# Low part of x^T and state update of the attention tiles: from VectorE subtractions and additions to identity products on TensorE and copies on ScalarE

## The chip, the cores and the metric

One core of one Trainium2 chip runs the whole program in one launch. The metric is device time in microseconds, the median of three runs. TensorE (PE) has a queue of its own for products and can load the next stationary operand while a product runs; VectorE (DVE), ScalarE (ACT) and GpSimd (POOL) each work through one queue in order; SyncE (SP) issues the DMAs.

## The reference, cut to what matters

Three layers follow each other over 1536 tokens of width 320: a gated linear attention, a feed-forward layer with a piecewise activation, and eight gated experts.

```python
for t in range(S):                       # S = 768, B = 2, H = 8, D = 40
    m_new = maximum(f[t] + m, i[t])
    f_stab, i_stab = exp(f[t] + m - m_new), exp(i[t] - m_new); m = m_new
    C = f_stab * C + i_stab * outer(v[t], k[t])
    n = f_stab * n + i_stab * k[t]
    y[t] = sigmoid(o[t]) * (C @ q[t]) / maximum(abs(n @ q[t]), 1)
x = y as [1536, 320]
h = x @ w_in;  g = where(h >= 1, h, where(h <= -1, 0, (h + 1)**2 / 4));  x = g @ w_out
P = exp(x @ w_gate - max), then 8 row and column normalisations
out = sum over e of P[:, e] * (maximum(x @ w1[e], 0) @ w2[e])
```

## The kernel before, in words

The attention runs in 12 tiles of 128 tokens (6 chunks of the sequence times 2 batches; tile t is chunk t // 2 of batch t % 2). A tile is a Python generator, `attn` (L357 to L452), that hands control back after each of its steps: the scaled values (POOL, L365), for each half of the heads the score products (L379), the decay scan (DVE, L383) and its product with the scores (DVE, L385), then the products with the old state (L395) and with the values (L400), then the outer products of this chunk for the new state (L407), then the division (L428 to L433), and at the end the transposes (L446) and the split of x^T.

The large products run in float32r, a one-record form of a float32 product in which an operand keeps fewer bits. So each operand is kept as a high part, rounded to that form, and a low part, the rest: `XH` and `XL` hold x^T so. `split_x` (L112 to L116) makes them from a PSUM bank: ACT copies to `XH`, DVE subtracts `XH` from the bank into `XL`. Products of plain float32 operands run as two records each.

The state `Cst` of a batch is scaled by the chunk's decay on POOL (L412); then two DVE additions, each of 40 partitions by 164 elements (L440), add the outer products from PSUM. In the first chunk two ACT copies (L442) set it.

Tiles 0 and 1 run first, side by side (L481 to L491), with four dummy products (`warm`, L296) after each step of each tile. The feed-forward layer runs in four stages (`STAGES`); the first is tokens 0 to 255, then 256 to 511, on the first half of the hidden width in pieces of 256 columns, and tiles 2 to 7 are worked off inside it; tiles 8 to 11 follow inside the next two stages. How many steps of a tile follow each piece of the layer is set by `RATE`; a tile needs 8 such steps. All through the first two stages the layer's weights arrive as 64-bit floats and are decoded with four DVE instructions each (`decode`, L213 to L220) and split like x^T. The experts follow.

`bank` hands out PSUM banks by tag: two for `at` (scores, values, outer products), one for `ax` (the product with the state, then the transposes of the same tile). The order of the instructions in each engine's queue is set at build time by the framework's planner with its own estimate of durations, not by the order of the program alone; in the trace, dummy products of later steps run ahead of products that had to wait. Inside stages 1 to 3 the attention's PE and DVE instructions are held behind named instructions of the layer.

Of the kernel before, what the change touches and what calls it, by code (L numbers as in the profile page):

```python
# [9 lines left out]
F32R = mybir.dt.float32r  # L10
I32 = mybir.dt.int32
U32 = mybir.dt.uint32
ACTF = mybir.ActivationFunctionType
ALU = mybir.AluOpType
# [20 lines left out]
WA, WG = 4, 2  # L35
PUMP = (0, 2, 4, 5, 6, 7, 10, 12, 13)
GP = 8
RATE = ((3.4, 0), (0, 2.25), (0, 2.25), (2, 2))

STAGES = ((0, (0,), 256), (512, (0, 1), 512), (0, (1,), 512), (1024, (0, 1), 512))  # L40
LAG1, LAG2 = 2, 3
# [7 lines left out]
def mlstm_moe_moe_kernel(  # L49
# [14 lines left out]
    mm = nc.tensor.matmul  # L64
    act = nc.scalar.activation
    vec = nc.vector
# [8 lines left out]
    def bank(tag):  # L75
        n = {"g1": 2, "g2": 3, "at": 2, "ax": 1}[tag]
        return ps.tile([128, 512], F32, name="bk_" + tag, tag=tag, bufs=n)
# [3 lines left out]
    XH = perm.tile([128, 3, NTOK], F32R, name="XH")  # L81
    XL = perm.tile([128, 3, NTOK], F32R, name="XL")
    ident = cst[:, C_ID : C_ID + 128]
    neg_dn = cst[:, C_ND : C_ND + 1]

    def f(ap):
        return ap.bitcast(F32)
# [24 lines left out]
    def split_x(planes, cols):  # L112
        for k, x in planes:
            act(out=XH[:, k, cols], in_=x, func=ACTF.Copy)
        for k, x in planes:
            vec.tensor_tensor(out=XL[:, k, cols], in0=x, in1=f(XH[:, k, cols]), op=ALU.subtract)  # L116
# [9 lines left out]
    with ExitStack() as atx:  # L126
        ap = atx.enter_context(tc.tile_pool(name="ap", bufs=1))
# [153 lines left out]

        g_s = ap.tile([32, L], F32R, name="g_s")
        zer = cst[0:32, 32 : 32 + L]
        m16_r = ap.tile([32, 16], F32R, name="m16_r")
        lend = ap.tile([104, NCH * 8], F32, name="lend")
        gt = ap.tile([128, NCH, 32], F32, name="gt")
        Cst = ap.tile([104, B, 4, 82], F32, name="Cst")
# [12 lines left out]
        for kw in kws:  # L300
            gp.memset(kw, 0.0)
        gp.memset(Cst, 0.0)
        act(out=m16_r, in_=cst[0:32, C_M16 : C_M16 + 16], func=ACTF.Copy)

        def gate_exps(a, b):
# [51 lines left out]
        def attn(t, tags):  # L357
            ta, tb = tags
            c, b = divmod(t, 2)
# [4 lines left out]
            vw = ap.tile([128, 8, 41], F32, name="vw", tag="vw", bufs=2)  # L364
# [3 lines left out]
            kw = kws[t == 1]  # L368
            for hf in range(2):
                gh = G[:, hf * 4 : hf * 4 + 4, :].rearrange("p h t -> p (h t)")  # L370
                gin = gh
                if c == 0:
                    gin = bank(ta)
                    for i in range(4):
                        h = b * 8 + 2 * i + hf
# [11 lines left out]
            if not last:  # L387
                gp.tensor_tensor(
                    out=kw.rearrange("p (i r) d -> p r i d", r=2)[:, :, :, 0:40], in0=kk.rearrange("p (i r) d -> p r i d", r=2),
                    in1=G[:, :, 127:128].rearrange("p (r i) d -> p r i d", r=2).to_broadcast([128, 2, 4, 40]), op=ALU.mult,  # L390
# [10 lines left out]
            sg = ap.tile([128, 384], F32, name="sg", tag="sg", bufs=2)  # L401
            act(out=sg[:, 0:320], in_=kvo_t[:, 648:968], func=ACTF.Sigmoid)
            yield
            if not last:
                pu = bank(ta)
                for pr in range(4):
                    mm(  # L407
                        pu[0:104, pr * 82 : (pr + 1) * 82], kw.rearrange("p h d -> p (h d)")[:, pr * 128 : pr * 128 + 104],
                        vw[:, 2 * pr : 2 * pr + 2, :].rearrange("p a d -> p (a d)"), start=True, stop=True,
                    )  # L410
                if c:
                    gp.tensor_tensor(  # L412
                        out=Cst[:, b, :, :], in0=Cst[:, b, :, :],
                        in1=lend[:, c * 8 + b * 4 : c * 8 + b * 4 + 4].unsqueeze(2).to_broadcast([104, 4, 82]), op=ALU.mult,
                    )
            pav = pa[:, 0:328].rearrange("p (h d) -> p h d", h=8)
            if c:
                hv = ap.tile([128, 8, 41], F32, name="hv", tag="hv")
                vec.tensor_tensor(
                    out=hv, in0=pi[:, 0:328].rearrange("p (h d) -> p h d", h=8),  # L420
                    in1=gt[:, c, 16 + b * 8 : 16 + b * 8 + 8].unsqueeze(2).to_broadcast([128, 8, 41]), op=ALU.mult,
# [13 lines left out]
            if not last:  # L435
                puv = pu[0:104, 0:328].rearrange("p (r d) -> p r d", r=4)
                for par in range(2):
                    rs, es = slice(par * 64, par * 64 + 40), slice(par * 41, par * 41 + 41)
                    if c:
                        vec.tensor_tensor(out=Cst[rs, b, :, es], in0=puv[rs, :, es], in1=Cst[rs, b, :, es], op=ALU.add)  # L440
                    else:
                        act(out=Cst[rs, b, :, es], in_=puv[rs, :, es], func=ACTF.Copy)  # L442
            px = bank(tb)
            act(out=sg[:, 320:384], in_=sg[:, 256:320], func=ACTF.Copy)
            for k in range(3):
                nc.tensor.transpose(px[:, k * 128 : (k + 1) * 128], sg[:, k * 128 : (k + 1) * 128], ident)  # L446
            yield
            split_x([(slice(0, 3), px[:, 0:384].rearrange("p (k t) -> p k t", k=3))], slice(t * 128, (t + 1) * 128))
            if t + 2 < NTILE:
                tiles_in[t + 2] = load_tile(t + 2)  # L450
            done.add(t)
# [4 lines left out]
        def attn_rest():  # L456
            g = attn(2, ("at", "ax"))
            next(g)
            for t in range(2, NTILE):
                n = 0  # L460
                nxt = None
                while next(g, g) is not g:
                    n += 1
                    if n == 6 and t + 1 < NTILE:
                        nxt = attn(t + 1, ("at", "ax"))
                        next(nxt)
                    yield
                g = nxt
# [4 lines left out]
        def pump_w():  # L473
            w_state[0] = next(wjobs, 99)
# [4 lines left out]
        gate_by_token(0, 1)  # L479
        gate_exps(L, S)  # L480
        starts = [attn(0, ("at", "ax")), attn(1, ("g2", "g2"))]  # L481
        step = 0
        while len(done) < 2:
# [88 lines left out]
        for si, (t0, hfs, w) in enumerate(STAGES):  # L572
# [7 lines left out]
            for hf in hfs:  # L580
# [10 lines left out]
                for o in range(0, 512, w):  # L591
                    while len(done) * 128 < t0 + o + w:
                        next(rest)
                    for ff in range(hf * 8, hf * 8 + 8, nf):
# [12 lines left out]
                        if w_state[0] < (9, 18, 18, 18)[si]:  # L607
                            pump_w()
                        credit += nf * RATE[si][hf]
                        while credit >= 1:  # L610
# [98 lines left out]
        for e in range(NE):  # L709
# [3 lines left out]
            for j in range(3):  # L713
# [17 lines left out]
                for i in range(4):  # L731
                    t = j * 4 + i
# [6 lines left out]
                    if e == NE - 1:  # L739
                        c, b = divmod(t, 2)  # L740
# [63 lines left out]
```

## Time and profile before

| | |
|---|---|
| median of 3 runs | 995.2 us (994.61 to 996.29) |
| the profiled execution's own time | 994.85 us |
| its span, first to last instruction | 993.1 us |
| PE busy | 979.6 us (99%) |
| PE weight loads busy | 861.8 us (87%) |
| DVE busy | 470.1 us (47%) |
| ACT busy | 344.8 us (35%) |
| POOL busy | 31.2 us (3%) |

The profile is of one execution. Its busy time of PE is modelled: products overlap in the array, so that records of 0.28 us follow each other every 0.12 us. How much of a stretch PE really needs is better seen in the distance from one product's start to the next. Shares over the whole span mix the attention with the experts, which take the last 690 us.

### The profile page before, as it was taken

The numbers are of one execution on the slowest core, as the hardware profiler recorded it, in microseconds if no ns is written. First come the engines' busy times: TensorE is split into PE (matmuls) and PEld (weight loads), VectorE is DVE, ScalarE is ACT, GpSimd is POOL, SyncE is SP. The second block draws the span as 40 slices with busy tenths as digits, with TensorE's granted clock in tenths as the row PEclk, the third lists the DMA queues.
The fourth block names the chain that finished last, engine by engine and source line by source line (L and its number), as shares of the span: only waits on it lengthen the run. The fifth ranks groups of instructions, "written<-read, shape, count | busy, mean of one in ns | idle before, by whom it ended". The sixth has DMA issues, their size and how long they took to land.

```text
span 993.1 us, 13483 instructions
## 1 busy us (share of the span) xinstructions
PE 979.6 (99%) x5520; PEld 861.8 (87%) x5520; DVE 470.1 (47%) x853; ACT 344.8 (35%) x622; POOL 31.2 (3%) x43
## 2 busy tenths in 40 slices
PE   9999899999999999999999999999999999999998
PEld 5789788887878899999999999989999999999997
DVE  9999977655563644322522432242253234222222
ACT  3743684477773224211411321141132123111111
POOL 2212101000000000000000000000000000000000
PEclk9999999999999999999999999999999999999999
DMA  5865413000132002100400210030021002000000
GB/s 171 263 169 172 143 57 99 12 1 0 47 113 75 1 1 64 54 1 1 117 1 1 74 44 1 7 111 1 1 87 31 1 17 72 1 1 1 27 27 27
DMA packets 42190, 51.91 MB, mean 52 GB/s; under 512 B 3360, under 2 KB 35744, under 8 KB 42128
## 3 DMA queue, kind: packets, MB, share of 16 engines
q1 hardware_dynamic: 42128, 51.05, 17.3%
q8 instruction: 43, 0.70, 0.3%
q14 instruction: 19, 0.16, 0.0%
HBM read 49.03 MB, written 2.01 MB: 51 GB/s over the span
## 4 chain that ended last, share of the span: by engine, by line
PE 89%; DVE 5%; ACT 3%; DMA 1%; issue 1%; SPq 0%; DVEq 0%; ACTq 0%
PE bk_g L124 41%; PE bk_g L704 9%; PE bk_g L706 8%; PE bk_g L705 8%; PE bk_ax L705 3%; PE bk_ax L704 3%; PE bk_ax L706 3%; PE bk_at L400 2%; PE bk_g L296 2%; PE bk_g L559 2%; PE bk_g L558 1%; PE bk_g L557 1%; PE bk_at L379 1%; DMA raw<-in_w_dram 1%; PE bk_g L561 1%
## 5 line engine op out<-in xcount | busy, mean ns | idle before, releaser
L124 PE MATMUL bk_g<-XH,wk 128*128 128x512 f32 (+1 forms) x1240 | 399.8, 388 | 1.6 <-DVE gs L545 1.6
L724 DVE SCALAR_TENSOR_TENSOR lo<-bk_g,hi 128x512 fp32r<-128x512 f32 x192 | 132.6, 691 | 372.6 <-ACT hi L723 371.7
L124 PE MATMUL bk_g<-XL,wk 128*128 128x512 f32 (+1 forms) x744 | 285.4, 384 | 0.0
L723 ACT ACTIVATE hi<-bk_g 128x512 fp32r<-128x512 f32 x192 | 114.9, 599 | 453.2 <-PE bk_g L124 453.0
L124 PEld LDWEIGHTS bk_g<-XH,wk 128*128 128x128 f32 x1240 | 230.6, 188 | 45.1 <-DVE gs L545 2.6
L704 PE MATMUL bk_g<-wf,hi 128*128 128x320 f32 x576 | 177.4, 308 | 1.1 <-ACT hi L723 1.1
L705 PE MATMUL bk_g<-wf,hi 128*128 128x320 f32 x576 | 177.0, 307 | 0.0
L706 PE MATMUL bk_g<-wf,lo 128*128 128x320 f32 x576 | 176.9, 308 | 0.0
L124 PEld LDWEIGHTS bk_g<-XL,wk 128*128 128x128 f32 x744 | 140.0, 188 | 21.4
L704 PEld LDWEIGHTS bk_g<-wf,hi 128*128 128x128 f32 x576 | 108.0, 187 | 8.1 <-ACT hi L723 1.6
L705 PEld LDWEIGHTS bk_g<-wf,hi 128*128 128x128 f32 x576 | 108.1, 188 | 6.3
L706 PEld LDWEIGHTS bk_g<-wf,lo 128*128 128x128 f32 x576 | 107.9, 187 | 0.0
L705 PE MATMUL bk_ax<-wf,hi 128*128 128x320 f32 x192 | 59.1, 308 | 0.0
L704 PE MATMUL bk_ax<-wf,hi 128*128 128x320 f32 x192 | 59.0, 307 | 0.0
L706 PE MATMUL bk_ax<-wf,lo 128*128 128x320 f32 x192 | 58.4, 304 | 0.0
L545 DVE TENSOR_TENSOR gs<-bk_g,gs 128x512 f32<-128x512 f32 x40 | 27.5, 688 | 26.8 <-ACT gs L543 26.4
L541 ACT ACTIVATE gs<-bk_g 128x512 f32<-128x512 f32 x48 | 28.5, 594 | 28.7 <-PE bk_g L124 28.1
L738 DVE SCALAR_TENSOR_TENSOR acc<-bk_g,P,acc 128x320 f32<-128x320 f32 x63 | 30.8, 545 | 15.3 <-PE bk_g L706 15.3
L531 DVE TENSOR_TENSOR wf<-raw,wf 128x640 fp32r<-128x640 f32 x32 | 26.3, 826 | 20.7 <-ACT wf L530 20.5
L704 PEld LDWEIGHTS bk_ax<-wf,hi 128*128 128x128 f32 x192 | 36.1, 188 | 0.0
L706 PEld LDWEIGHTS bk_ax<-wf,lo 128*128 128x128 f32 x192 | 36.1, 188 | 0.0
L705 PEld LDWEIGHTS bk_ax<-wf,hi 128*128 128x128 f32 x192 | 35.9, 187 | 0.0
(198 smaller groups left out, 999.6 us busy)
## 6 DMA issues: line engine op xcount, KB each, us to landing
raw<-in_w_dram SPq DMA_DIRECT2D x32, 320.0 KB
raw<-in_w_dram SPq DMA_DIRECT2D x32, 256.0 KB
kvo_t<-in_kvo_dram SPq DMA_DIRECT2D x12, 484.0 KB
raw<-in_w_out_dram SPq DMA_DIRECT2D x8, 640.0 KB
raw<-in_w_in_dram SPq DMA_DIRECT2D x8, 512.0 KB
raw<-in_w_dram SPq DMA_DIRECT2D x64, 64.0 KB
qk<-in_qk_dram SPq DMA_DIRECT2D x24, 160.0 KB
G<-g_d SPq DMA_DIRECT2D x5, 512.0 KB
```

The source lines that it names most:

```text
L124: return [mm(dst, a, b, start=i == 0, stop=i == len(seq) - 1) for i, (a, b) in enumerate(seq)]
L296: mm(to, wz, wz[:, 0:1].to_broadcast([128, 512]), start=True, stop=True)
L400: mm(pa[:, h * 41 : (h + 1) * 41], A[h % 2][:, h // 2, :], vw[:, h, :], start=True, stop=True)
L531: vec.tensor_tensor(out=wf[:, fs, 320:640], in0=rs[n], in1=f(wf[:, fs, 0:320]), op=ALU.subtract)
L541: act(out=t, in_=pg, func=ACTF.Relu, scale=-1.0, bias=1.0)
L545: dve_at.append(vec.tensor_tensor(out=g, in0=pg, in1=t, op=ALU.max))
L704: mm(pp[i], hi[:, ts], wf[:, ff, 0:320], start=st, stop=False)
L705: mm(pp[i], hi[:, ts], wf[:, ff, 320:640], start=False, stop=False)
L706: mm(pp[i], lo[:, ts], wf[:, ff, 0:320], start=False, stop=sp)
L723: act(out=hi, in_=pg, func=ACTF.Relu)
L724: vec.scalar_tensor_tensor(out=lo, in0=pg, scalar=0.0, in1=f(hi), op0=ALU.max, op1=ALU.subtract)
L738: vec.scalar_tensor_tensor(out=acc[:, t, :], in0=pp[i], scalar=P[:, t, e : e + 1], in1=acc[:, t, :], op0=ALU.mult, op1=ALU.add)
```

## The change

Three things are made in another way, for each attention tile:

- The low part of x^T. The transposes and the ACT copy to `XH` stay. After one more hand-over of control, three plain float32 products of `sg` with the identity write x^T into the same bank again, a float32r product of the negated identity (`nid`, new, made once by ACT) with `XH` is added to it, and ACT copies the bank to `XL`.
- The update of the state, from the second chunk on. The decayed state is multiplied by the identity into the bank of the outer products as the first product of the group, the four outer products are added to it, and ACT copies the sum back in two pieces. The scaling on POOL now stands ahead of these products in the program.
- A tile has one step more (9 in place of 8 after the first), and `RATE` is raised to 3.75 and 2.5 steps. In the start each step brings its four dummy products for each tile. The dummies inside the tiles are unchanged.

```diff
-RATE = ((3.4, 0), (0, 2.25), (0, 2.25), (2, 2))
+RATE = ((3.75, 0), (0, 2.5), (0, 2.5), (2, 2))
@@
+        nid = ap.tile([128, 128], F32R, name="nid")
@@
+        act(out=nid, in_=ident, func=ACTF.Copy, scale=-1.0)
@@ attn
                 pu = bank(ta)
-                for pr in range(4):
-                    mm(
-                        pu[0:104, pr * 82 : (pr + 1) * 82], kw...[:, pr * 128 : pr * 128 + 104],
-                        vw[:, 2 * pr : 2 * pr + 2, :]..., start=True, stop=True,
-                    )
                 if c:
                     gp.tensor_tensor(
                         out=Cst[:, b, :, :], in0=Cst[:, b, :, :],
                         in1=lend[...]..., op=ALU.mult,
                     )
+                    mm(pu[0:104, 0:328], ident[0:104, 0:104], Cst[:, b].rearrange("p r d -> p (r d)"), start=True, stop=False)
+                for pr in range(4):
+                    mm(
+                        pu[0:104, pr * 82 : (pr + 1) * 82], kw...[:, pr * 128 : pr * 128 + 104],
+                        vw[:, 2 * pr : 2 * pr + 2, :]..., start=c == 0, stop=c == 0 or pr == 3,
+                    )
@@
                     rs, es = slice(par * 64, par * 64 + 40), slice(par * 41, par * 41 + 41)
-                    if c:
-                        vec.tensor_tensor(out=Cst[rs, b, :, es], in0=puv[rs, :, es], in1=Cst[rs, b, :, es], op=ALU.add)
-                    else:
-                        act(out=Cst[rs, b, :, es], in_=puv[rs, :, es], func=ACTF.Copy)
+                    act(out=Cst[rs, b, :, es], in_=puv[rs, :, es], func=ACTF.Copy)
@@
             yield
-            split_x([(slice(0, 3), px[:, 0:384].rearrange("p (k t) -> p k t", k=3))], slice(t * 128, (t + 1) * 128))
+            ts, p3 = slice(t * 128, (t + 1) * 128), px[:, 0:384].rearrange("p (k t) -> p k t", k=3)
+            act(out=XH[:, :, ts], in_=p3, func=ACTF.Copy)
+            yield
+
+            for k in range(3):
+                mm(px[:, k * 128 : (k + 1) * 128], sg[:, k * 128 : (k + 1) * 128], ident, start=k == 0, stop=False)
+            mm(px[:, 0:384], nid, XH[:, :, ts], start=False, stop=True)
+            act(out=XL[:, :, ts], in_=p3, func=ACTF.Copy)
```

## Rows read from the trace of the kernel before

**Rows 1.** The page's head: span, then busy time, share and instructions of an engine.
```profile
span 993.1 us, 13483 instructions
PE 979.6 (99%) x5520; PEld 861.8 (87%) x5520; DVE 470.1 (47%) x853; ACT 344.8 (35%) x622; POOL 31.2 (3%) x43
```

**Rows 2.** Busy time of each engine by stretch, up to the attention's end.
```profile
core 0: us, PE busy (x) PEld busy (x) DVE busy (x) ACT busy (x) POOL busy (x), PEclk, DMA share, GB/s
0.00:36.30 36.30, 35.10 (x202) 21.45 (x202) 34.19 (x66) 17.36 (x35) 6.99 (x17) 1.00 0.64 183
36.30:118.60 82.30, 77.82 (x604) 70.70 (x603) 77.44 (x150) 39.84 (x80) 19.45 (x20) 0.98 0.64 188
118.60:141.90 23.30, 21.87 (x98) 17.81 (x98) 22.27 (x43) 21.59 (x43) 0.00 (x0) 1.00 0.22 71
141.90:175.00 33.10, 31.64 (x189) 27.14 (x188) 21.69 (x37) 15.91 (x28) 4.76 (x6) 1.00 0.30 90
175.00:230.20 55.20, 55.20 (x286) 46.26 (x285) 31.32 (x56) 32.35 (x57) 0.00 (x0) 1.00 0.01 4
```

**Rows 3.** Groups on PE in 36.3 to 118.6 us: line, form, count, busy, mean.
```profile
L124 PE MATMUL bk_g<-XH,wk 128*128 128x256 f32 x80 | 18.0, 304 | 0.0
L124 PE MATMUL bk_g<-XL,wk 128*128 128x256 f32 x48 | 14.1, 298 | 0.0
L379 PE MATMUL bk_at<-qk 104*128 104x128 f32 x96 | 12.8, 281 | 0.0
L400 PE MATMUL bk_at<-vw,A 128*128 128x41 f32 x96 | 11.9, 277 | 0.1
...
L296 PE MATMUL bk_at<-wz 128*128 128x512 bf16 x24 | 6.4, 380 | 0.2 <-DVE A L385 0.2
...
L296 PE MATMUL bk_g<-wz 128*128 128x512 bf16 x16 | 5.5, 412 | 0.8 <-DVE XL L547 0.8
...
L446 PE MATMUL bk_ax<-cst,sg 128*128 128x128 f32 x18 | 3.6, 285 | 0.9 <-DVE sg L433 0.9
```

**Rows 4.** Chain of work, 0 to 130 us: start, us, engine, tile, line, records.
```profile
81.50 0.89 PE bk_at L379 x8
...
82.63 0.33 PE bk_ax L446 x3
...
84.54 0.85 PE bk_ax L395 x8
85.39 0.99 PE bk_g L124 x8
...
88.23 0.77 PE bk_at L407 x8
...
105.63 0.87 PE bk_at L296 x4
106.50 1.73 PE bk_at L400 x16
...
116.06 0.47 PE bk_g L124 x2
```

**Rows 5.** Waits of PE's products, 36.3 to 118.6 us: total, times, longest.
```profile
PE bk_g L557 <- ACT XH L546: 2.1, 2, 1.9
PE bk_ax L446 <- DVE sg L433: 0.9, 2, 0.5
```

**Rows 6.** Copies and subtractions out of bank `ax`: min/median/max ns.
```profile
L114 ACT ACTIVATE XH<-bk_ax x11: 491/491/493, 34.8 to 211.7; 128x384 fp32r<-128x384 f32 x11
L116 DVE TENSOR_TENSOR XL<-bk_ax,XH x11: 531/549/558, 36.3 to 212.2; 128x384 fp32r<-128x384 f32 x11
```

**Rows 7.** Writers of the state: min/median/max ns, first and last start.
```profile
L440 DVE TENSOR_TENSOR Cst<-bk_at,Cst x16: 307/326/331, 53.5 to 174.4; 40x164 f32<-40x164 f32 x16
L412 POOL TENSOR_TENSOR Cst<-Cst,lend x8: 728/732/1202, 42.4 to 172.7; 104x328 f32<-104x328 f32 x8
L442 ACT ACTIVATE Cst<-bk_at x2: 304/306/307, 27.8 to 28.1; 40x164 f32<-40x164 f32 x2
```

More of the change, by code (lines that the diff above doesn't have):

```diff
@@ L405, in attn @@
                 pu = bank(ta)
-                for pr in range(4):
-                    mm(
-                        pu[0:104, pr * 82 : (pr + 1) * 82], kw.rearrange("p h d -> p (h d)")[:, pr * 128 : pr * 128 + 104],
-                        vw[:, 2 * pr : 2 * pr + 2, :].rearrange("p a d -> p (a d)"), start=True, stop=True,
-                    )
                 if c:
@@ L414, in attn @@
                         in1=lend[:, c * 8 + b * 4 : c * 8 + b * 4 + 4].unsqueeze(2).to_broadcast([104, 4, 82]), op=ALU.mult,
+                    )
+                    mm(pu[0:104, 0:328], ident[0:104, 0:104], Cst[:, b].rearrange("p r d -> p (r d)"), start=True, stop=False)
+                for pr in range(4):
+                    mm(
+                        pu[0:104, pr * 82 : (pr + 1) * 82], kw.rearrange("p h d -> p (h d)")[:, pr * 128 : pr * 128 + 104],
+                        vw[:, 2 * pr : 2 * pr + 2, :].rearrange("p a d -> p (a d)"), start=c == 0, stop=c == 0 or pr == 3,
                     )
```

## The prediction

> **What bounds the kernel now.** I began with the head of the page [rows 1]: PE is busy for 979.6 of 993.1 us. For the experts I take that as it stands, since nothing of the change reaches them. For the attention I asked for the busy time by stretch [rows 2]. The reader is to see two engines that are nearly full at the same time in 36.3 to 118.6 us, the first stage of the layer with tiles 2 to 7 in it: DVE is busy for 77.44 of 82.3 us, PE for a modelled 77.82. The change takes from the one and gives to the other, so all depends on how much of PE is free there.
>
> The modelled busy time can't say it. I count instead: how many records PE has in the stretch, and how far apart their starts lie when nothing holds them up. The chain of waits gives the distances [rows 4]: 0.87/4 = 0.217 us for a dummy, 0.99/8 = 0.124 us for a float32r product of 256 columns (0.12 in denser places), and for one record of a plain float32 product 0.89/8 = 0.111 (128 columns), 1.73/16 = 0.108 (41 columns), 0.85/8 = 0.106 and 0.77/8 = 0.097 (82 columns). The stretch has 604 product records [rows 2]. Of these 24 + 16 are dummies [rows 3]: 40 x 0.217 = 8.7 us. The other 564 lie between 0.097 and 0.124 us; at 0.114, with about half of them float32r, they are 64.3 us. PE needs 73.0 of 82.3 us, and 9.3 us are slack. Of the slack 1.6 us are clock: the granted clock is 0.98 of full over the stretch, against 1.00 in its neighbours [rows 2]. The named waits in it lead to DVE, directly or over an ACT copy of its output [rows 5].
>
> After 118.6 us PE is plainly the bound: busy for 21.87 + 31.64 + 55.20 = 108.7 of 111.6 us up to the attention's end, 2.9 us idle, none of it after 175 us [rows 2].
>
> The Trainium skill ("Perfetto Trace Analysis", Identifying the Most-Contended Engine) calls matmul busy time a bad measure of how full TensorE is, and asks for the busy share of the weight loads; for VectorE it takes the busy share itself. By that rule PE stands at 70.70/82.3 = 86% in the stretch, with 11.6 us free, and DVE at 94% is the engine to relieve: the change would then pay, as in the first rival. The count above says 9.3 us where the rule says 11.6. I go by the count.
>
> **The change part by part.** Removed from DVE: a subtraction of 0.549 us for each of 12 tiles [rows 6] and two additions of 0.326 us for tiles 2 to 9 [rows 7]. In the first stage that is 8 x 0.549 + 12 x 0.326 = 8.3 us of 77.4 (the subtractions of tiles 0 and 1 fall at its start); later 4 x 0.549 + 4 x 0.326 = 3.5 us. DVE's records overlap a little, so this is the most that DVE can gain.
>
> Added to PE, for each of 12 tiles: three plain float32 products of 128 columns, two records each, 6 x 0.111 = 0.67 us; and a float32r product of 384 columns, half-way between 0.12 (256) and 0.235 (512) [rows 4], 0.18 us. Together 0.84 us a tile, 10.1 us.
>
> Added to PE for tiles 2 to 9: a plain float32 product of 328 columns. The trace has none so wide. Below, it can't beat two float32r passes: 328/512 x 0.235 x 2 = 0.30 us. Above, if a record's 0.111 us at 128 columns were all streaming, 2 x 0.111 x 328/128 = 0.57 us; that 41 columns take 0.108 us too says that part of it is the weight load. I take 0.57, since the nearest row is the plain float32 one, and keep 0.30 for the range. 8 x 0.57 = 4.6 us.
>
> Added to PE in the start: one step more, 2 x 4 dummies x 0.217 = 1.7 us.
>
> In all PE gets 10.1 + 4.6 + 1.7 = 16.4 us. By place:
> - Before the first layer product, tiles 0 and 1: 1.7 + 1.7 = 3.4 us. In 0 to 36.3 PE shows 1.2 us idle [rows 2]. I let all of it be filled: 2.2 us later.
> - First stage, tiles 2 to 7: 6 x 0.84 + 6 x 0.57 = 8.5 us on 9.3 us of slack. PE's need goes to 81.5 us and becomes what sets the stage's length; DVE's goes to about 69. So PE's gaps, which lead back to a late DVE, should mostly close. A full queue never closes them all: I let three quarters close, 7.0 us. Net 1.5 us later.
> - Later stages, tiles 8 to 11: 4 x 0.84 + 2 x 0.57 = 4.5 us against 2.9 us of idle time, of which I let 2.0 be filled. Net 2.5 us later.
>
> Sum: 2.2 + 1.5 + 2.5 = 6.2 us.
>
> ACT gets a copy of 0.49 us a tile [rows 6] and two of 0.306 for tiles 2 to 9 [rows 7]. In the first stage it is busy for 39.84 of 82.3 us, and 8 x 0.49 + 12 x 0.31 = 7.6 us fit beside PE. In 118.6 to 141.9 it is at 21.59 of 23.3, but no tile ends there (POOL, which starts each tile, is idle) [rows 2]. Cost nothing; without that cover each late copy would hold the PE product behind it. The negated identity is one more ACT copy in the first microseconds, before any step needs it: nothing.
>
> New waits. The identity product of the state stands behind POOL's scaling, 0.73 us [rows 7]; in PE's queue the value products, 1.73 us [rows 4], stand ahead of it and cover that. If POOL is late, the four outer products and all the layer products behind them wait. The bank `ax` is held longer: after the `XH` copy come 0.84 us of products and a 0.49 us copy, where there was one subtraction of 0.55, so some 0.8 us more before the next tile's state product may start. The planner can put layer products in between; where it can't, PE stands. I count it at nothing in the sum and in full in the last rival. The new step count, 9 against 8, goes with `RATE` 3.75 against 3.4: tiles per layer piece 0.417 against 0.425, no change worth a number.
>
> The profiled execution took 994.85 us; 994.85 + 6.2 = 1001.0 us. The median of the runs is 0.35 us above that execution, which is less than any term here; I keep 1001.0.
>
> **The rivals.**
> 1. DVE is the bound, and PE's added work falls into gaps. For it: DVE's 94% in the first stage [rows 2], and PE's named waits, which lead to DVE [rows 5]. Against it: the count, by which PE has no room for 8.5 us and a stage shortened by DVE's 8.3 us at once. It decides where the wide product costs 0.30 us and the three products a tile overlap so well that PE needs under about 74 us in that stage: then DVE's relief shows, 8.3 x 0.7 = 5.8 us off, and the later stages give back 4.5 - 2.9 = 1.6. Some 4 us faster: 991 us. Chance 0.17.
> 2. The costs and the slack cancel: every gap closes, 16.4 - (1.2 + 9.3 + 2.9) = 3.0, and the wide product costs 0.30 us, 8 x 0.27 = 2.2 less. That is 0.8 us slower, 995.7 us, which can't be told from no change. Chance 0.23.
> 3. A wait takes the place of the one removed: PE stands at the bank `ax` or behind a late `XH` copy. It takes 12 turns of ACT, PE, ACT; at 0.5 us each 6 us more: 1007 us. For it: PE's longest wait in the first stage is already one on an ACT copy, 1.9 us, and the clock fell in that stage [rows 2, 5]. Against it: less work on DVE makes these copies earlier. Chance 0.20.
>
> The Trainium skill ("Perfetto Trace Analysis", Transposes) asks that a transposition be issued as a transpose, not as a standard matmul. The trace agrees: three transposes took 0.33 us [rows 4], and the three products that repeat them are to take 0.67. [...]
>
> **How the numbers follow.** The forecast, 998 to 1004 us, has 0.40; rivals 1, 2 and 3 have 0.17, 0.23 and 0.20. A measurement of this kernel tells about 0.2%, 2 us, from no change. Faster by more than that is rival 1: 0.17. Within it is rival 2: 0.23. Slower is the forecast and rival 3: 0.60. The range, 993 to 1007 us, leaves out most of rival 1 and the upper tail of rival 3.
>
> **What would show it.** Right: DVE's busy time falls by some 8 us up to the first stage's end; PE has 8 x 7 + 6 x 2 = 68 more records by then beside 8 more dummies; the held copies (L635 before, at 118.6 us) come 3 to 4 us later; the state products of 328 columns are over 0.25 us apart; the attention's last transposes come some 6 us later. Wrong: those held copies come earlier, which is rival 1; or PE shows more named waits on ACT than the 2.1 us of now, which is rival 3. What would upset the sum as a whole is a planner that orders the first stage quite differently, so that PE's slack was another one than counted.

## The result, and the profile after

The changed kernel took 1007.97 us (median of 4 runs, 1007.23 to 1011.12) beside 995.75 us of the kernel before (4 runs): 1.0121 times as long, 95% interval 1.0093 to 1.0149. That is 12.2 us more. The forecast was 1001.0 us with a range of 993 to 1007: the direction was right, the amount was half of what came, and the time lies just outside the range. Medians and ratios, here and in the experiments, leave out one execution of c_only that took 2510 us.

The profiled execution took 1007.23 us, its span is 1005.5 us. PE is busy for 993.6 us of it, 99% as in [rows 1], DVE for 462.3, 46% where it was 47%. Busy time by stretch, cut where the stages now end, answers to [rows 2]:

```profile
core 0: us, PE busy (x) PEld busy (x) DVE busy (x) ACT busy (x) POOL busy (x), PEclk, DMA share, GB/s
0.00:40.20 40.20, 38.63 (x222) 24.03 (x226) 37.43 (x72) 20.20 (x42) 8.12 (x18) 1.00 0.66 193
40.20:126.40 86.20, 83.16 (x649) 75.96 (x655) 80.79 (x150) 48.27 (x103) 17.66 (x19) 1.00 0.62 182
126.40:149.50 23.10, 21.87 (x99) 17.75 (x98) 10.23 (x18) 18.52 (x34) 0.00 (x0) 1.00 0.11 32
149.50:184.00 34.50, 32.81 (x195) 27.84 (x194) 21.69 (x34) 15.82 (x31) 4.93 (x6) 1.00 0.26 79
184.00:243.10 59.10, 59.10 (x311) 49.85 (x312) 29.06 (x49) 34.53 (x62) 0.00 (x0) 1.00 0.00 1
```

The reader is to see three things against [rows 2]. The time came in three parts: 3.9 us before the first layer product, 82.3 to 86.2 = 3.9 us in the first stage, 111.6 to 116.7 = 5.1 us after it; the rest of the span is 0.5 us shorter. The granted clock of the first stage is 1.00 where it was 0.98. And DVE, relieved of 20 instructions in that stage, is still busy for 80.79 of 86.2 us, 94% as before.

Where did DVE's freed time go? To weight decoding drawn forward. Its last instruction, first in the kernel before and then in the changed one (count, min/median/max ns, first and last start):

```profile
L220 DVE SCALAR_TENSOR_TENSOR raw<-raw,dv x18: 675/686/828, 21.4 to 138.6; 128x512 int32<-128x512 int32 x10, 128x640 int32<-128x640 int32 x8
```

```profile
L220 DVE SCALAR_TENSOR_TENSOR raw<-raw,dv x18: 676/750/1246, 21.8 to 125.8; 128x512 int32<-128x512 int32 x10, 128x640 int32<-128x640 int32 x8
```

Before, 13 of the 18 pieces had come to it by 115.9 us and the last began at 138.6; now all of them have begun when the first stage ends. In the kernel before no named wait of PE's products in 36 to 250 us is for a decoded weight, so the decoding had not been late for them.

What TensorE got, in groups of 40.2 to 126.4 us (as [rows 3]; L297 are the dummies, L413 and L454 the new products with the identities) and in the chain of waits (as [rows 4]; L453 are the three products that repeat the transposes):

```profile
L297 PE MATMUL bk_at<-wz 128*128 128x512 bf16 x20 | 5.6, 379 | 0.8 <-DVE A L387 0.6
...
L413 PE MATMUL bk_at<-Cst,cst 104*104 104x328 f32 x12 | 4.7, 473 | 0.3 <-POOL Cst L409 0.3
...
L297 PE MATMUL bk_g<-wz 128*128 128x512 bf16 x13 | 4.1, 380 | 0.2
...
L297 PEld LDWEIGHTS <-wz 128*128 128x128 bf16 x38 | 3.8, 106 | 2.3 <-issue 0.6
...
L454 PE MATMUL bk_ax<-XH,nid 128*128 128x384 f32 x6 | 2.5, 421 | 0.0
```

```profile
76.74 0.61 PE bk_at L413 x2
...
108.83 0.68 PE bk_ax L453 x6
```

So 0.68 us for the three repeated products (0.67 reckoned) and 0.61 us for the wide one (0.57 reckoned). The float32r product of 384 columns starts at 68.40 us in the timeline and the next record at 68.66: 0.26 us, where 0.18 was reckoned. A tile brings 0.94 us, the whole change 12 x 0.94 + 8 x 0.61 + 1.7 = 17.9 us of TensorE.

The same count as in the prediction, with the changed records. Of the dummies only 20 + 13 product records stand in the trace, but 38 of their weight loads, as many as in the kernel before, where 40 products stand beside them: some records are missing, and 40 dummies ran. They are 8.7 us; 6 wide products, 3.7; 6 products of 384 columns, 1.6; the other 649 - 33 - 12 - 6 = 598 records at 0.114, 68.2. TensorE needs 82.2 of 86.2 us, 9.2 more than before; 4.0 us are slack, of which nothing is clock. Before it was 9.3, of which 1.6 was clock. So 5.3 us of the added work found room in this stage. The named waits of PE in the stretch, to set beside [rows 5]:

```profile
PE bk_ax L446 <- DVE sg L436: 1.4, 3, 0.8
PE bk_at L297 <- DVE A L387: 0.6, 1, 0.6
PE bk_at L413 <- POOL Cst L409: 0.3, 1, 0.3
PE bk_ax L446 <- ACT sg L444: 0.2, 1, 0.2
```

The 1.9 us wait on an ACT copy is gone, and no new one of that kind has come.

### The profile page after: what moved, and what is told of

It is laid out like the page before. It is cut to its first block, busy times and chain, and to the rows that moved or that the text cites. A ratio compares the mean times of both kernels' runs of the same rounds, so it can differ in the third digit from the quotient of the medians.

```text
span 1005.5 us, 13684 instructions
## 1 busy us (share of the span) xinstructions
PE 993.6 (99%) x5617; PEld 874.3 (87%) x5628; DVE 462.3 (46%) x825; ACT 354.9 (35%) x651; POOL 30.7 (3%) x43
## 4 chain that ended last, share of the span: by engine, by line
PE 89%; DVE 5%; ACT 3%; DMA 1%; issue 1%; SPq 0%; POOL 0%; DVEq 0%; ACTq 0%
PE bk_g L124 41%; PE bk_g L711 8%; PE bk_g L713 8%; PE bk_g L712 8%; PE bk_ax L712 3%; PE bk_ax L711 3%; PE bk_ax L713 3%; PE bk_at L402 2%; PE bk_g L564 2%; PE bk_g L566 2%; PE bk_g L565 2%; PE bk_at L381 1%; DMA raw<-in_w_dram 1%; PE bk_g L297 1%; PE bk_g L567 1%
```

## The experiments

Theory 1: the time up to the attention's end is TensorE's work plus gaps of its own that VectorE's load hardly changes, so added products are paid nearly in full. Theory 2: VectorE's queue, kept full by decoding, makes the gaps. Theory 3: the longer chain through bank `ax` makes TensorE wait.

The granted clock turned out to differ from kernel to kernel. At 1.2 GHz in place of 2.4 TensorE takes nearly twice as long: in 68.4 to 69.6 us of the kernel before, where the granted clock is 0.50, the layer's products of 256 columns start 0.21 us apart, against 0.124 [rows 4]. So the table gives beside the measured time also the time at full clock: each run's time less (1 - granted clock) times its span, median. This takes off the most that the half clock can have cost, since it counts as lost also what TensorE spent waiting at half clock. For the kernel before it is 993.9 to 994.3 us in every set of the experiments; differences in the last column are against that. Ratios are to the kernel before on the same chip.

| kernel | us | ratio, 95% interval | mean clock | at full clock |
|---|---|---|---|---|
| changed kernel | 1007.97 | 1.0121 (1.0093 to 1.0149) | 0.999 | +13.8 |
| no_products | 997.9 | 1.0019 (1.0008 to 1.003) | 0.996 | +0.2 |
| x_only | 1009.37 | 1.0127 (1.011 to 1.0143) | 0.995 | +10.3 |
| c_only | 1004.6 | 1.0084 (1.0067 to 1.0101) | 0.996 | +7.3 |
| c_again | 1011.02 | 1.0142 (1.0115 to 1.0169) | 0.988 | +5.9 |
| step_only | 1000.87 | 1.0044 (1.003 to 1.0058) | 0.996 | +2.0 |
| before_nodec | 993.98 | 0.998 (0.9962 to 0.9997) | 0.997 | -2.5 |
| after_nodec | 1006.69 | 1.0092 (1.0065 to 1.0119) | 0.998 | +10.7 |
| after_held | 1016.87 | 1.0189 (1.0162 to 1.0216) | 0.995 | +16.9 |
| before_wa8 | 1002.31 | 1.0063 (1.0042 to 1.0084) | 0.999 | +7.1 |
| before_wa2 | 996.72 | 1.0007 (0.9997 to 1.0016) | 0.996 | -2.1 |
| before_wa0 | 998.28 | 1.0003 (0.9988 to 1.0019) | 0.993 | -4.3 |
| after_wa0 | 1006.21 | 1.0093 (1.0069 to 1.0117) | 0.997 | +8.7 |
| x_pool | 1000.19 | 1.0032 (1.0014 to 1.0049) | 0.996 | +2.9 |
| before_wd2 | 1006.39 | 1.0081 (1.0058 to 1.0103) | 0.984 | -5.0 |
| after_nid3 | 1014.15 | 1.0149 (1.012 to 1.0178) | 0.997 | +16.1 |

The sum hides where the time goes. By stretch, in the profiled execution of each kernel (us, granted clock in brackets):

| kernel | to the first layer product | first stage | then, to the attention's end |
|---|---|---|---|
| before | 36.3 (1.00) | 82.3 (0.98) | 111.6 (1.00) |
| changed kernel | 40.2 (1.00) | 86.2 (1.00) | 116.7 (1.00) |
| no_products | 38.8 (1.00) | 78.4 (1.00) | 115.3 (0.99) |
| x_only | 40.2 (1.00) | 83.7 (1.00) | 121.2 (0.96) |
| step_only | 38.0 (1.00) | 82.4 (0.98) | 113.4 (1.00) |
| before_nodec | 36.3 (1.00) | 80.6 (0.96) | 115.3 (0.97) |
| after_nodec | 39.7 (1.00) | 83.3 (1.00) | 119.5 (0.97) |
| after_held | 40.2 (1.00) | 87.0 (1.00) | 121.9 (0.97) |
| before_wa8 | 36.3 (1.00) | 82.9 (1.00) | 116.6 (1.00) |

These are single executions, and a new plan can move a stage by some microseconds, so single differences are rough.

**no_products: the relief alone.** The outer products, with `start=True, stop=True` again, write the bank by themselves:

```diff
-                    mm(pu[0:104, 0:328], ident[0:104, 0:104], Cst[:, b]..., start=True, stop=False)
-            for k in range(3):
-                mm(px[:, k * 128 : (k + 1) * 128], sg[:, k * 128 : (k + 1) * 128], ident, start=k == 0, stop=False)
-            mm(px[:, 0:384], nid, XH[:, :, ts], start=False, stop=True)
```

> The changed kernel without any of its identity products: XL is copied straight from the transposes and the state straight from the outer products (so the low part of x^T is x^T itself and the decayed state is left out of the update). VectorE keeps its relief of 8.3 us in the first stage, TensorE gets only the 1.7 us of dummies of the extra step. Theory 1, TensorE's gaps are its own and relief of VectorE is worth nothing: before plus 1 to 3 us, the held copies at 118 to 121 us. The forecast's own step, three quarters of the gaps close when VectorE is relieved: 5 to 7 us below before, held copies near 113 us. Theory 3, the longer chain through bank ax costs: no such chain here, so no word beyond theory 1.

Measured: +2.1 us, +0.2 at full clock. The held copies came at 117.2 us, earlier than theory 1 had them and far from 113. The first stage and what follows it:

```profile
38.80:117.20 78.40, 75.07 (x602) 68.80 (x601) 72.56 (x134) 45.43 (x95) 17.47 (x20) 1.00 0.69 201
117.20:232.50 115.30, 110.42 (x570) 92.37 (x569) 69.86 (x119) 72.55 (x135) 5.39 (x6) 0.99 0.12 35
```

Inside the first stage the relief does show: 78.4 us, 3.9 less than before, of which 1.6 is clock; the forecast let 7.0 go. It is given back outside: 2.5 us before the first layer product, where the extra step brings 1.7 us of dummies, and 3.7 us after the stage, where TensorE has as many records as before. Why the later stages grew isn't shown. In the total, with 1.7 us of dummies added, the relief is worth some 1.5 us at full clock, less than the noise between two plans (3 us, see the parts).

**x_only, c_only, c_again, step_only: the parts.** x_only takes the first hunk of the change with the new step and `RATE`, c_only the state's hunk alone, c_again is c_only once more, and step_only has the new `RATE` and this in place of `split_x`:

```diff
+            act(out=XH[:, :, ts], in_=p3, func=ACTF.Copy)
+            yield
+            vec.tensor_tensor(out=XL[:, :, ts], in0=p3, in1=f(XH[:, :, ts]), op=ALU.subtract)
```

> Only the low part of x^T in the new way, the state's update as before. TensorE gets 12 x (0.67 + 0.26) + 1.7 = 12.9 us. Theory 1 (time is TensorE's work, of which only the 1.7 us lost to the clock and some 2 us of gaps come back): before plus 8 to 11 us. Theory 3 (the chain transposes, copy, products, copy makes TensorE wait): nearly all of the loss is here, plus 11 to 12 us, with waits on ACT's copies of over 4 us in the first stage.

> Only the state's update in the new way, the low part of x^T and the number of steps as before. TensorE gets 8 x 0.58 = 4.6 us, VectorE loses 5.2. Theory 1: before plus 2 to 4.5 us. Theory 3: before plus 0 to 1 us, as the chain through bank ax is untouched. If VectorE were the bound of the first stage: before minus 2 or more.

> The kernel before with the added hand-over between the copy to XH and VectorE's subtraction, and the new RATE; no product added, VectorE's work as before. TensorE gets the 8 dummies, 1.7 us. Theory 1: before plus 1 to 2.5 us. Theory 3 says nothing more than that. If pacing or planning by the extra step cost much by itself: plus 4 us or more.

As measured, all three missed theory 1's bounds: x_only +13.6 (8 to 11 expected, 11 to 12 by theory 3), step_only +5.1 (1 to 2.5 expected, 4 or more if pacing or planning cost by itself), c_only +8.8 (2 to 4.5 expected). At full clock x_only costs 10.3 us for 13.0 of TensorE's work and step_only 2.0 for 1.7, as theory 1 has it; some 3 us of each measured time are clock. In x_only's first stage PE has no named wait on ACT, where theory 3 wanted over 4 us of them.

> The same kernel as c_only, for a profile that can be read: its time was 9.5 us above before where TensorE's added products are 4.6 us. Theory 1 leaves some 5 us to explain: they must show as half-clock stretches (1.7 us each) or as new waits of TensorE, on POOL's scaling, on the state's products or on ACT's copies. If neither shows, the gaps between products have grown everywhere.

In c_again (+14.8) most of it showed as clock. The first stage of its profiled execution:

```profile
36.80:130.60 93.80, 87.15 (x618) 77.95 (x617) 81.76 (x152) 46.05 (x97) 18.14 (x20) 0.91 0.60 178
```

With the stretch after it, 118.2 us at 0.96, that is 0.09 x 93.8 + 0.04 x 118.2 = 13 us lost to the half clock in that execution. Of c_only's own +8.8 only 1.5 is clock. TensorE's longest waits in c_again's first stage were 1.6 us for a masked score product (`A`) and 1.3 for an `XH` copy. At full clock the part costs 5.9 to 7.3 us, still more than its 4.9 us of products; the surplus of 1 to 2.4 us I can't place. The parts together, 10.3 + 6.6, are 3 us above the whole: each edit makes the planner order everything anew, and I take that as the noise of such a comparison.

**before_nodec, after_nodec: VectorE bound nowhere.**

```diff
-            vec.tensor_scalar(out=v, in0=v, scalar1=..., scalar2=..., op0=ALU.max, op1=ALU.min)
-            vec.tensor_scalar(out=v_i, in0=v_i, scalar1=3, scalar2=0x3FFFFFF8, ...)
-            vec.scalar_tensor_tensor(out=v_i, in0=lo_i, scalar=29, ...)
-            vec.scalar_tensor_tensor(out=hi_i, in0=hi_i, scalar=-0x40000000, ...)
```

> The kernel before with VectorE's four decode instructions of each weight piece left out (the weights are then other numbers): some 45 us of VectorE's work in the first 140 us are gone, so VectorE is bound nowhere. Theory 1, TensorE's work and its own gaps set the time: before minus 0 to 4 us. Theory 2, VectorE's full queue makes TensorE's gaps: most of 9.3 us in the first stage and 2.9 later come back, before minus 8 to 12 us.

> The changed kernel with the same decode instructions left out. Theory 1: 11 to 15 us above before_nodec, as the changed kernel stands to the one before. Theory 2 (the changed kernel stays slow because VectorE's freed time was filled with decoding drawn forward, 18 pieces by the end of the first stage against 13): within 6 us of before_nodec.

The first stage of before_nodec and of after_nodec:

```profile
36.30:116.90 80.60, 76.77 (x599) 71.42 (x598) 57.62 (x110) 35.22 (x70) 14.91 (x20) 0.96 0.62 187
```

```profile
39.70:123.00 83.30, 81.88 (x653) 75.33 (x652) 55.17 (x102) 49.19 (x104) 14.96 (x19) 1.00 0.65 194
```

DVE falls from 94% to 71% and 66% of the stage, and the total of the kernel before by only 2.2 us. The changed kernel stays 12.7 us behind (13.2 at full clock). For the total this decides between theories 1 and 2. The first stage does get shorter, by 1.7 us (0.04 x 80.6 = 3.2 more are clock) and by 2.9 in the changed kernel: VectorE's load makes a part of the gaps there.

**after_held: decoding kept out of the first stage.** The same hold is put on the decoding in the middle of the second stage.

```diff
                         if w_state[0] < (9, 18, 18, 18)[si]:
-                            pump_w()
+                            if si and w_state[0] >= 0:
+                                with tc.issue_after(dve_at[-2].ins):
+                                    pump_w()
+                            else:
+                                pump_w()
```

> The changed kernel with the decode of stage 1's pieces held on VectorE behind the layer's last maxima, so that it can't be drawn forward into the first stage. Theory 1: the first stage ends where it did, held copies at 125 to 128 us, total within 3 us of the changed kernel or above it. Theory 2: held copies at 122 us or earlier and 3 to 5 us off the total.

Held copies at 127.2 us (126.4 in the changed kernel). VectorE was busy for 63.6 of the first stage's 87.0 us, 73% in place of 94%, and the stage was 0.8 us longer: the decoding drawn forward did no harm there, and theory 2 has failed for the stage it was about. The total is 8.9 us above the changed kernel, 3.1 at full clock, which is no more than the noise of a new plan: in the profiled execution 5.2 us come between the stage and the attention's end, where the clock was 0.97, and 3.7 after that. What the hold itself cost isn't shown.

**before_wa8, before_wa2, before_wa0, after_wa0: TensorE time by itself.**

```diff
-            if 2 <= t < 8:
-                warm(WA, pa)
+            if 2 <= t:                       # before_wa8; wa2: WA = 2; wa0: both lines out
+                warm(8 if t < 8 else 4, pa)
```

> The kernel before with dummies added ahead of the value products, 4 more in each of tiles 2 to 7 and 4 in each of tiles 8 to 11, which wait for nothing of the new way: 40 x 0.217 = 8.7 us of TensorE's time, VectorE's and ScalarE's work unchanged. Theory 1 (added TensorE work is paid in full, whatever the other engines do): before plus 6 to 10 us. The forecast's step (gaps of 9.3 us in the first stage take most of the added work): before plus 2 to 4 us. Theory 3 (the waits of the new chain cost, not the work): before plus 0 to 3 us.

> The kernel before with two dummies in place of four in tiles 2 to 7: 2.6 us less on TensorE. Theory 1: before minus 1 to 2.5 us with the clock unchanged; if the clock falls more often, up to 3 us above.

> The kernel before without the dummies inside tiles 2 to 7: 24 x 0.217 = 5.2 us less on TensorE. Theory 1: before minus 3 to 5 us if the granted clock stays as it is; each microsecond at half clock takes half a microsecond back, so that 8 us more at half clock would leave only 1 us. VectorE as the bound of the first stage: no change within 1 us.

> The changed kernel without the dummies inside tiles 2 to 7. Theory 1: 3 to 5 us below the changed kernel, some 1003 us, with the same reserve on the clock. If the chain through bank ax sets the pace: no change within 1 us.

Measured, before_wa8 is 6.0 us slower, at the lower edge of theory 1's bounds and outside the others. The removals gave almost nothing to the kernel before (+0.5 for before_wa2, a ratio of 1.0003 for before_wa0) and 1.8 us to the changed one; for before_wa0 that is also what was expected if VectorE set the time. At full clock 8.7 us added cost 7.1; 2.6 taken away gave 2.1; 5.2 gave 4.3, and 5.0 in the changed kernel: some 80% either way, without any of the new chain, so that theory 3 isn't needed. For before_wa8, at a clock of 0.999, this hardly depends on the correction; for the removals it does. The first stage of before_wa8 and what follows it:

```profile
36.30:119.20 82.90, 79.42 (x624) 70.76 (x623) 79.18 (x156) 40.15 (x80) 17.43 (x20) 1.00 0.66 187
119.20:235.80 116.60, 113.32 (x589) 93.75 (x588) 73.92 (x129) 70.18 (x127) 4.77 (x6) 1.00 0.14 41
```

The 80% are a mean of two unlike parts. In the first stage 24 more dummies, 5.2 us, cost 0.6 us (2.2 with the 1.6 us of clock that came back): there most of the work fell into gaps, as the forecast's step has it. After the stage 16 dummies, 3.5 us, cost 5.0: no room shows there. The first stage of before_wa0:

```profile
36.50:119.50 83.00, 75.01 (x582) 70.20 (x581) 74.55 (x145) 38.17 (x76) 17.46 (x20) 0.94 0.63 181
```

The waits on the `XH` copies grew from 2.1 us [rows 5] to 3.8, the longest from 1.9 to 2.8, and the granted clock fell to 0.94: up to 0.06 x 83 = 5 us, as much as the dummies had cost.

**x_pool: relief in a kernel that computes the same.** GpSimd took the subtraction.

```diff
-            split_x([(slice(0, 3), px...)], slice(t * 128, (t + 1) * 128))
+            act(out=XH[:, :, ts], in_=p3, func=ACTF.Copy)
+            xf = sg.rearrange("p (k t) -> p k t", k=3)
+            act(out=xf, in_=p3, func=ACTF.Copy)
+            gp.tensor_tensor(out=XL[:, :, ts], in0=xf, in1=f(XH[:, :, ts]), op=ALU.subtract)
```

> The kernel before, with VectorE's subtraction for the low part of x^T moved to GpSimd: ScalarE copies the bank twice, once to XH and once to SBUF, and GpSimd subtracts there. VectorE loses the same 6.6 us over the attention as in the change, TensorE gets nothing. Theory 1: within 1.5 us of before. If VectorE's relief is worth anything by itself: 3 us or more below before.

+3.2 us by the ratio, outside the 1.5 us and the other way than relief would have it. GpSimd needed twice VectorE's 0.549 us [rows 6]:

```profile
L452 POOL TENSOR_TENSOR XL<-sg,XH x12: 1002/1162/1906, 35.8 to 217.3; 128x384 fp32r<-128x384 f32 x12
```

A layer product waited for it once, 1.0 us, and ScalarE has 12 copies more. So relief without added products gained nothing here either, but this run doesn't separate it from these costs.

**before_wd2: the dummies of the start.**

```diff
-WD = 4
+WD = 2
```

> The kernel before with two dummies in place of four after each step of tiles 0 and 1: 9 x 2 x 2 x 0.217 = 7.8 us less on TensorE before the first layer product. Theory 1 carried to the start (TensorE's 30.6 us of records fill 36.4 us): the first layer product comes 3 us or more earlier and the total falls by 2 to 4 us, less half of what comes at half clock. If the start is set by VectorE and the weights, so that the change's 3.8 us there have another cause than TensorE's dummies: first layer product within 1 us of 36.4, total within 1.5 us of before.

```profile
0.00:37.80 37.80, 30.78 (x168) 20.20 (x168) 32.96 (x65) 17.18 (x35) 6.84 (x17) 0.91 0.56 163
```

TensorE's longest named wait in that stretch:

```profile
PE bk_g L446 <- DVE sg L433: 3.7, 1, 3.7
```

Both expectations were missed. The first layer product came at 37.8 us, later than before, with the granted clock at 0.91, and TensorE, busy for 30.78 us, stood waiting for VectorE's divided values; in the kernel before no such wait shows, the dummies lie there. So TensorE's work does not set the start by itself. In the change some 1.7 us of the 3.9 came with the step and its dummies (first product at 38.0 us in step_only); the rest goes with the products of tiles 0 and 1 (40.2 in x_only). The total rose by 0.8%. The clock, 0.984 against 0.997, is enough for that, but the +8.3 us and the -5.0 at full clock only bound what the dummies were worth, since in the start TensorE was not full.

**after_nid3: the slow product of 384 columns.**

```diff
-            mm(px[:, 0:384], nid, XH[:, :, ts], start=False, stop=True)
+            for k in range(3):
+                mm(px[:, k * 128 : (k + 1) * 128], nid, XH[:, k, ts], start=False, stop=k == 2)
```

> The changed kernel with the product of the negated identity and XH, 384 columns in three pieces, 0.26 us start to start, issued as three products of 128 columns. If the pieces' distance in SBUF makes it slow: 3 x 0.06 to 0.08 us, 0.5 to 1 us off in all. If a float32r product of few columns costs as much as its weight load, 0.11 us each: 0.33 us a tile and up to 1 us more in all. Neither reaches 2 us of the total.

From the start of the first of the three products to the next record's it is 0.143 + 0.113 + 0.112 = 0.37 us a tile against 0.26: the one instruction is the better form. Up to 1 us was expected, +2.3 came at full clock, within the noise of a new plan. Whether the distance between the pieces is what makes the one instruction slow stays open.

## Why the prediction was half right

- **Which engine sets the time.** Right for the total, and shown: with 45 us of VectorE's work gone the kernel is 2.2 us faster, with 8.7 us of TensorE's work added 6.0 us slower. As a measure of room both shares said too much for the first stage: the count of starts had 9.3 us free there, the share of weight loads 11.6, and 5.3 were taken up.
- **The terms of added work.** Right but for one: 0.67 and 0.57 us measured as 0.68 and 0.61; the 384 columns took 0.26 us, not 0.18, 1.0 us over 12 tiles. In all 17.9 us where the prediction had 16.4. That the nearer bound for the 328 columns, 0.57, held and not 0.30 was a choice between two values that came out.
- **"I let all of it be filled", "I let three quarters close, 7.0 us", "of which I let 2.0 be filled".** This is the step that failed: TensorE's idle time was taken as room. By it 10.2 us of the added work were to vanish; 5.0 did, all of them in the first stage. Before the first layer product 3.6 us of work cost 3.9 (2.2 forecast). In the first stage 9.2 us cost 3.9 (1.5 forecast): 5.3 found room where 7.0 were let in, and 1.6 of these are the clock, which no longer fell. In the later stages 5.0 us cost 5.1 (2.5 forecast). Sum 6.2 against 12.9; of the 6.7 missing some 1.5 are the size of the terms, 1.7 the first stage and 3.5 the idle time of the other two places. The experiments say the same of the places: 1.7 us of dummies cost 1.7 to 2.5 before the first layer product (step_only, no_products), 5.2 us of them 0.6 in the first stage and 3.5 us 5.0 after it (before_wa8).
- **Why the gaps stay.** The argument was that they lead back to a late VectorE. In the changed kernel VectorE's queue stayed as full as before, with work that could wait. Where it was truly relieved, the first stage did get shorter, by 3.9 us (no_products) and 1.7 us (before_nodec), clock included, but the total fell by no more than 2.2 us. After the first stage VectorE is busy for only 61.0 of 116.7 us, and there the added work was paid in full; so a late VectorE is not what all the gaps have in common. What they consist of, apart from the named waits, isn't shown.
- **Rival 1** (VectorE is the bound) fell with no_products: all of the relief and none of the products, and not faster.
- **Rival 3** gave the nearest number, 1007 us, by a mechanism that isn't there: PE's named waits on ACT in the first stage are 0.2 us, none in x_only, and dummies that wait for no chain cost about the same share. That the number came near is luck.
- **What would show it.** The held copies came 7.8 us later (3 to 4 forecast), the last transpose at 223.3 us, 12 later (6 forecast); the records of 328 columns were 0.3 us apart, as forecast, and TensorE has the 68 + 8 more records up to the first stage's end (by the weight loads: 226 + 655 against 202 + 603). VectorE's busy time up to the first stage's end was to fall by 8 us; it rose, since the decoding was drawn forward.

## What to carry to other kernels

Where two engines are both near full, look at what the relieved engine will do next: if its queue holds work that can wait, it stays full, and the relief hardly shows, while the engine that takes the work over pays for it: here about four fifths of the work, over the whole. Count TensorE by the distance of its starts times its records, stage by stage, and don't take what is left for room until an experiment has put work there: dummies that wait for nothing of the change tell it for each stage. Before ranking variants, put each run's time and its granted clock side by side: here the clock can account for up to 16 us of a run (before_wd2).

## What the runs showed of the hardware that was not expected

- Taking dummies away made the kernel slower: with 7.8 us fewer in the start the granted clock of the runs was 0.984 on average, against 0.997 for the kernel before beside it, and the total rose by 0.8%.
- A plain float32 product of 328 columns takes two records of 0.305 us, about 0.93 ns a column and record; a float32r product of 512 columns takes 0.235 us [rows 4], 0.46 ns a column; the float32r one over three separate pieces of 128 columns took 0.26 us, 0.68 ns a column.
- A float32 subtraction of 128 by 384 elements took GpSimd 1.16 us (both operands in SBUF, x_pool) and VectorE 0.55 (one in PSUM).
